# One half of the query-state product copied out of PSUM by ScalarE, the second mask built later, and a new order on all engines, in a layer of Hedgehog linear attention and a dense block

## Chip, cores and metric

The kernel runs on one core of one Trainium2 chip. The metric is the device time of one execution in microseconds. A core has TensorE (PE), VectorE (DVE), ScalarE (ACT), GpSimd (POOL) and SyncE (SP, which here only issues DMAs); each takes its instructions in order and waits on semaphores for the others.

## The reference, cut to what matters

```python
def _A_ref(x, wqkv, w_phi, wo):                   # x: 1 x 2048 x 640, 32 heads of 20
    q, k, v = split((x @ wqkv))                   # each 32 heads x 2048 x 20
    pq = einsum("bhsd,hdf->bhsf", q, w_phi)
    pk = einsum("bhsd,hdf->bhsf", k, w_phi)
    phi_q = concat([softmax(pq), softmax(-pq)])   # 40 features
    phi_k = concat([softmax(pk), softmax(-pk)])
    kv = einsum("bhsf,bhsd->bhfd", phi_k, v)      # one 40 x 20 state per head
    z  = einsum("bhsf->bhf", phi_k)
    num = einsum("bhqf,bhfd->bhqd", phi_q, kv)
    den = einsum("bhqf,bhf->bhq", phi_q, z)[..., None] + 1e-6
    return (num / den) joined over heads @ wo

h  = x + _A_ref(layernorm(x), A_wqkv, A_w_phi, A_wo)
h2 = h + silu(layernorm(h) @ B_w1) @ B_w2         # 640 -> 1728 -> 640
```

Inputs and weights are bf16. The attention is not causal: all keys go into one state per head before any query is answered.

## The kernel before

The 2048 tokens are 16 tiles of 128. Token tiles form four groups of four for the transposed activations XnT and EqT, and five groups (0-1, 2-5, 6-9, 10-13, 14-15) for the dense block. All work is cut into small words, such as `dp.3` (an operation and its tile), and one string, ORDER, lists them. Each word calls a function `op_<name>`, whose instructions are appended to the queues of the engines that they use. So each engine runs the words that concern it in the order of the string, nothing is reordered, and the semaphores are placed by the layer below, from what each instruction reads and writes. The number behind an `@` is the PSUM bank (of eight) where a word's product starts; letters at the end choose an engine (`v` VectorE, `a` ScalarE, `p` GpSimd; `q` and `b` split a kn between GpSimd and VectorE). DMAs go out on SyncE's queue (`.s`) or ScalarE's (`.a`).

The start: lx, lk, lp, lv load x, the key and value weights and w_phi. wm is a run of matmuls on constants; wt transposes a piece of the key weights on TensorE, wc copies it out; ph makes a block-diagonal form of w_phi with a first mask (mk); fk multiplies the two into Wfk, and fc (ScalarE) copies it out. mc builds a second mask, maskR, on GpSimd (a memset and four selects, lines 207 to 215); mo writes ones into the ten Vp tiles; mt transposes maskR into maskS on VectorE and copies a column of it into KVBD on GpSimd.

Key and value stage, for each tile: st takes the statistics (VectorE), rs the reciprocal root (GpSimd, lines 272 to 283), xn normalizes, xt and xc transpose by TensorE or xd by a DMA. kp and vp multiply with Wfk and the value weights (line 364); ke takes both exps (ScalarE), kr the sums and reciprocals (VectorE), kn normalizes (GpSimd, in part VectorE), vc copies the values out, and cc adds the tile into the state, which stays in PSUM bank 7. gk and gc make Wfq as fk and fc make Wfk, from transposed query weights (lq). When the last cc is done, kc copies the state out, VectorE transposes it (KVF), and km masks it into KVBD.

Query stage: qp multiplies Wfq with a group's XnT (10 matmuls of 512 columns, or 5 where there is a single row block), qe takes both exps from PSUM into EqT (ScalarE, line 461), and dp multiplies EqT with KVBD into four PSUM banks: 40 matmuls in strips of 32 rows (line 486). The result holds the positive half A[0] and the negative half A[1] side by side in each of these banks. dw then combines them, and stands unchanged in both kernels; before, every dw has `how="p"`:

```python
    def op_dw(t, how="p"):
        ...
        nc.vector.reciprocal(w[:], A[1][:, :, :, 21])                                  # L500
        nc.vector.tensor_tensor(w[:], w[:], A[0][:, :, :, 21], op=ALU.mult)            # L501
        if how == "c":
            kept = wk2().tile([P, 4, 8, 21], F32, name="kept", bufs=1)
            nc.scalar.copy(kept[:], first)                                             # L504
            first = kept[:]
        ...
        nc.vector.tensor_tensor(u[:], A[1][:, :, :, 0:21], w..., op=ALU.mult)          # L507
        nc.vector.tensor_tensor(u[:], u[:], first, op=ALU.add)                         # L510
```

Here `first` is A[0] in PSUM. dr takes the reciprocal of the denominators (rd, line 515), do multiplies each half of the heads by it (line 521, VectorE or GpSimd), td transposes the result by a DMA, op multiplies with wo, oa adds the residual (line 557), sq takes the sum of squares (ScalarE), sr the statistics (GpSimd, five or six small instructions), hn normalizes, hd transposes by a DMA.

Dense block, by group: up multiplies with w1 into two banks, ua takes Silu on ScalarE (line 649, with a table load before the first), yp and yh multiply with w2, yo and yz add the residual and store.

Of the kernel before, what the change touches and what calls it, by code (L numbers as in the profile page):

```python
# [30 lines left out]
rs.3.4 st.10 vc.1.a xn.3.v xn.8.a vp.0@0 vc.0.a vp.2@4 vc.2.a xt.3@2 xc.3.a xn.9.v st.11 rs.10.12 xn.11.a
lx.4.8.s kp.2@6 st.7 ke.2 vp.3@0 lx.12.16.s kp.3@4 ke.3 xd.9 kp.9@2 st.6 xd.8 vp.8@6 xn.10.v rs.6.8 vc.3.a
xd.10 xn.6.a lq.4.s st.4 st.5 rs.4.6 xn.4.a ke.9 xn.5.a kr.0 kr.1 kn.0.p vp.9@4 vc.9.a kp.8@0 kn.1.p xd.11
vc.8.a st.13 xn.7.a kr.9 kn.9.p kp.10@2 ke.10 st.12 rs.12.14 kr.3 kn.3.p ke.8 vp.10@4 vc.10.a xd.6 kr.8
kn.8.p vp.6@6 vc.6.a kr.2 lq.3.s xn.13.a vp.11@2 vc.11.a xd.4 vp.4@0 vc.4.a kp.4@4 lq.2.s gk.2@6 st.15 xd.5
gk.1@2 kp.5@0 st.14 xd.7 ke.4 kr.4 gc.2.a xn.12.a kp.6@4 cc.3 gc.1.a ke.5 cc.0 ke.6 cc.8 cc.9 rs.14.16
xn.14.a mt kr.5 cc.1 kn.2.q lq.0.s xd.13 kp.13@2 ke.13 kr.13 l1.0.s l1.1.s vp.5@0 vc.5.a xn.15.v kr.10 xd.12
kn.5.p kn.13.q vp.13@4 vc.13.a xd.14 kp.12@2 ke.12 kr.12 kn.10.p kp.11@0 ke.11 kr.6 vp.7@4 vc.7.a gk.4@2
vp.12@0 kn.4.q l2.0.2.s l2.2.4.s gc.4.a gk.3@4 gc.3.a kp.14@2 vp.14@4 vc.14.a kn.12.p cc.2 cc.5 kr.11 ke.14
cc.4 cc.10 vc.12.v kr.14 kn.11.q xd.15 kp.15@4 ke.15 kp.7@2 lo.0.2.s lo.2.5.s kn.14.p gk.0@0 gc.0.a kr.15  # L40
# [5 lines left out]
do.4.0.p qe.2.2 qp.3.2@5 op.1@6 qe.3.2 dp.5@0 oa.1 sq.1 l2.8.10.s l2.10.13.s op.2@4 qp.3.1@6 qe.3.1 dw.5.p
do.4.1.p td.4 sr.1 dp.9@0 hn.1.v lh.s oa.2 dr.5 dw.9.p do.5.0.p sq.2 op.3@4 oa.3 do.5.1.p op.4@6 oa.4 dp.7@0
dw.7.p dr.7 hd.1 up.0.2@4 ua.0.2 dr.6 up.0.3@6 ua.0.3 do.6.0.v dr.9 sq.4 dp.8@0 do.6.1.p up.0.1@4 ua.0.1
do.9.0.p dw.8.p sq.3 dr.8 sr.2 hn.2.a td.5 op.5@6 do.8.1.p oa.5 do.8.0.v sq.5 dp.13@0 dw.13.p up.0.0@4
ua.0.0 td.6 op.6@6 do.9.1.v oa.6 hd.2 dp.12@0 dr.13 do.7.1.v sr.4 hn.4.a sr.5 yp.1.0@4 sr.3 td.9 yp.0.1@6  # L50
dw.12.p hn.3.a td.8 do.7.0.p td.7 yh.0.0 hd.4 hn.5.v hd.5 do.13.1.p dp.11@0 dw.11.p dr.11 hd.3 yp.0.0 yo.0
yp.1.1 yo.1 op.7@0 dp.15@2 oa.7 dr.12 do.12.0.v sq.7 sr.7 op.8@6 sq.6 oa.8 do.13.0.v sr.6 hn.6.a op.9@0 oa.9
td.13 dw.15.p do.12.1.p td.12 up.1.0@6 dr.15 do.15.0.v up.1.6@0 ua.1.0 ua.1.6 dp.10@2 sq.9 hn.7.v do.15.1.v
td.15 sr.9 hn.9.v hd.9 up.1.4@6 ua.1.4 dw.10.p dr.10 do.10.0.p hd.6 up.1.3@0 op.12@6 ua.1.3 op.13@2 oa.13
do.10.1.p op.15@4 sq.8 td.10 up.1.2@0 oa.12 hd.7 sr.8 do.11.1.v hn.8.v ua.1.2 up.1.1@2 ua.1.1 hd.8 up.1.5@6
ua.1.5 up.2.6@0 oa.15 dp.14@2 dw.14.p up.2.3@6 ua.2.6 sq.13 up.2.2@0 ua.2.2 do.11.0.v sq.15 sq.12 td.11
op.10@2 oa.10 up.2.1@4 ua.2.1 dr.14 do.14.0.v up.2.5@0 ua.2.5 yp.5.0@2 ua.2.3 up.2.0@4 sr.12 hn.12.v ua.2.0
hd.12 sr.13 hn.13.a op.11@0 oa.11 hd.13 sr.15 hn.15.v up.2.4@6 hd.15 sq.10 sr.10 hn.10.a ua.2.4 yp.2.0@4
yp.4.0@0 sq.11 yp.3.1@6 sr.11 yh.1.0 hd.10 hn.11.v hd.11 yh.1.1 yp.4.1 yo.4 yp.2.1 yo.2 yp.5.1 up.3.3@0
yp.3.0 ua.3.3 do.14.1.p td.14 up.3.2@4 ua.3.2 op.14@0 oa.14 yo.5 up.3.0@4 yo.3 up.3.6@0 yh.2.1@2,6 ua.3.0  # L60
ua.3.6 up.3.4@4 sq.14 sr.14 hn.14.a hd.14 yp.9.0 yp.9.1 yo.9 up.3.5@0 ua.3.5 up.3.1@6 yp.6.0@0 ua.3.4 ua.3.1
yp.12.0@4 yp.12.1 yp.10.1@6 yp.7.1 yp.7.0 yo.7 yp.6.1 yh.2.0@2 yo.6 yh.3.0 yp.8.0 yp.8.1 yo.8 up.4.2@0
ua.4.2 up.4.1@2 ua.4.1 yo.12 up.4.0@4 yp.11.0@0 ua.4.0 up.4.3@2 ua.4.3 yp.14.0@4 yp.15.1@2 yp.10.0 yo.10
yp.14.1 yp.15.0 yh.4.0 yo.15 yo.14 yh.3.1@6,7 yp.11.1 yo.11 yp.13.0 yz.13.0.s yp.13.1 yz.13.1.a
"""

@with_exitstack
def kernel(
# [448 lines left out]

    def op_do(t, a, eng):
        if ("o", t) not in tl:
            tl["o", t] = wk2().tile([P, D], BF16, name="o", bufs=5)  # L520
        (nc.vector if eng == "v" else nc.gpsimd).tensor_tensor(  # L521
            tl["o", t][:, a * 320 : (a + 1) * 320].rearrange("p (h f) -> p h f", f=DH),
            tl["u", t][:, a, :, 0:DH],
            tl["rd", t][:, a, :].unsqueeze(2).to_broadcast([P, 16, DH]),
            op=ALU.mult,
        )
# [213 lines left out]
```

## Time and profile before

| what | value |
|---|---|
| median of 3 runs | 239.14 us (238.87 to 239.17) |
| the profiled execution, its own time | 238.86 us |
| its span, first to last instruction | 237.2 us |
| busy: PE, DVE, ACT, POOL | 229.9, 133.7, 114.9, 92.9 us |
| granted TensorE clock | 1.00 |
| first kp / first dp / first up / first yp | 10.65 / 69.27 / 96.37 / 108.0 us |

Stages by the span: start until 10.65 us, keys and values until about 67, queries and the attention's output overlapping the dense block from about 96, dense block to the end. Busy times overlap between engines. A line of the chain gives start, length and what ran; a group of instructions gives the line, the engine, the operation, tiles, shapes and count, then busy time and mean nanoseconds, then the engine's idle time before it with its releaser.

### The profile page before, as it was taken

To read this page: it belongs to the slowest core of one execution; us is meant where nothing else is said; L and a number is where in the kernel's file an instruction comes from. 1 tells how busy PE (TensorE), PEld (TensorE's weight loads), DVE (VectorE), ACT (ScalarE), POOL (GpSimd) and SP (SyncE) were. 2 spreads that over 40 slices of the span, in tenths; PEclk is the share of its full clock that TensorE was granted. 3 is DMA by queue.
4 is the path that set the end of the run, shared out by engine and by line. 5 is a ranking of instruction groups with operands and counts; after the bars stand their busy time and mean duration, and the time that the engine had idled before them with its cause. 6 is when DMAs were issued, how large, how long until landed. Compare 5 with 4: busy or idle time off the path is not lost.

```text
span 237.2 us, 6320 instructions
## 1 busy us (share of the span) xinstructions
PE 229.9 (97%) x2672; PEld 147.6 (62%) x2672; DVE 133.7 (56%) x257; ACT 114.9 (48%) x172; POOL 92.9 (39%) x184
## 2 busy tenths in 40 slices
PE   6899999999999999999999999999999999999995
PEld 2677777777544555886754645556654657688762
DVE  3899999899838989988878504321203000220032
ACT  3788998866866575664054254654014240013000
POOL 7656897798923454188071600534000100000000
PEclk9999999999999999999999999999999999999999
DMA  7964768495001849123734411103211100020012
GB/s 209 305 239 92 128 118 184 120 249 175 3 6 31 179 80 197 37 53 62 113 83 86 83 30 28 29 12 75 72 41 55 28 28 3 28 83 3 0 60 83
DMA packets 44845, 20.68 MB, mean 87 GB/s; under 512 B 34448, under 2 KB 44304, under 8 KB 44816
## 3 DMA queue, kind: packets, MB, share of 16 engines
q1 hardware_dynamic: 43728, 19.88, 36.1%
q10 hardware_dynamic: 1088, 0.39, 0.7%
q8 instruction: 21, 0.34, 0.6%
q14 instruction: 8, 0.07, 0.1%
HBM read 9.61 MB, written 2.62 MB: 52 GB/s over the span
## 4 chain that ended last, share of the span: by engine, by line
PE 88%; DVE 4%; POOL 4%; ACT 1%; DMA 1%; issue 1%; DVEq 0%; POOLq 0%
PE mm L673 24%; PE mm L627 23%; PE mm L364 18%; PE mm L548 8%; PE mm L451 7%; PE mm L486 3%; PE mm L420 2%; ACT EqT L461 1%; DMA X<-in_A_x_dram 1%; PE mm L686 1%; DVE u L507 1%; DVE u L510 1%; PE mm L637 1%; POOL RS L275 1%; PE mm L331 1%
## 5 line engine op out<-in xcount | busy, mean ns | idle before, releaser
L627 PE MATMUL mm<-HnT,w 128*128 128x512 bf16 (+1 forms) x325 | 59.1, 337 | 0.0
L649 ACT ACTIVATE shT<-mm 128x1024 bf16<-128x1024 f32 (+2 forms) x29 | 27.7, 963 | 64.3 <-PE mm L627 48.8
L673 PE MATMUL mm<-w,shT 128*128 128x320 bf16 (+2 forms) x416 | 58.5, 299 | 0.0
L673 PEld LDWEIGHTS <-shT 128*128 128x128 bf16 x416 | 39.7, 98 | 17.7 <-issue 0.8
L627 PEld LDWEIGHTS <-w 128*128 128x128 bf16 x325 | 31.3, 98 | 22.8 <-issue 0.3
L694 DVE TENSOR_TENSOR ob<-mm,X 128x640 bf16<-128x640 f32 x15 | 12.0, 817 | 47.0 <-PE mm L673 29.3
L364 PEld LDWEIGHTS <-XnT 128*128 128x128 bf16 x320 | 30.7, 98 | 11.8 <-issue 0.2
L407 POOL TENSOR_TENSOR Ek<-Ek,Sk 128x1280 bf16<-128x1280 bf16 (+2 forms) x16 | 34.6, 2184 | 3.1 <-DVE Sk L400 2.2
L557 DVE SCALAR_TENSOR_TENSOR X<-mm,X 128x640 bf16<-128x640 f32 x16 | 13.1, 823 | 21.5 <-PE mm L548 21.3
L397 DVE TENSOR_REDUCE Sk<-Ek 128x64 f32<-128x1280 bf16 x16 | 23.3, 1456 | 1.6 <-ACT Ek L389 1.6
L548 PE MATMUL mm<-wo,ot 128*128 128x320 bf16 x160 | 23.9, 299 | 0.2 <-ACT EqT L461 0.2
L521 POOL TENSOR_TENSOR o<-u,rd 128x320 bf16<-128x320 f32 x20 | 14.7, 752 | 22.7 <-DVE rd L515 14.4
L364 PE MATMUL mm<-Wfk,XnT 128*128 128x320 bf16 x160 | 23.4, 299 | 0.0
L451 PE MATMUL mm<-XnT,Wfq 128*128 128x512 bf16 x100 | 23.3, 380 | 0.0
L461 ACT ACTIVATE EqT<-mm 128x1024 bf16<-128x1024 f32 (+1 forms) x24 | 19.6, 884 | 7.4 <-PE mm L451 7.4
L364 PE MATMUL mm<-wv,XnT 128*128 128x320 bf16 x160 | 23.2, 299 | 0.0
L389 ACT ACTIVATE Ek<-mm 128x640 bf16<-128x640 f32 x32 | 20.6, 710 | 3.2 <-PE mm L364 2.7
L548 PEld LDWEIGHTS <-ot 128*128 128x128 bf16 x160 | 15.4, 98 | 7.4 <-issue 0.7
L565 ACT ACTIVATE sq<-X 128x640 bf16<-128x640 bf16 x16 | 11.7, 730 | 9.3 <-DVE X L557 7.7
L267 DVE BATCH_NORM_STATS2 stats<-X 128x6 f32<-128x320 bf16 x32 | 13.7, 468 | 3.8 <-DMA X<-in_A_x_dram 3.8
L577 POOL TENSOR_SCALAR hm<-hst,hm 128x1 f32<-128x1 f32 x16 | 4.6, 290 | 28.0 <-ACT sq L565 27.0
L451 PEld LDWEIGHTS <-Wfq 128*128 128x128 bf16 x100 | 9.1, 98 | 9.9
(78 smaller groups left out, 214.0 us busy)
## 6 DMA issues: line engine op xcount, KB each, us to landing
out_dram<-ob SPq DMA_DIRECT2D x15, 160.0 KB, 1.8
w<-in_B_w_dram SPq DMA_DIRECT2D x6, 360.0 KB, 5.2
X<-in_A_x_dram SPq DMA_DIRECT2D x3, 640.0 KB, 6.6
...
```

The source lines that it names most:

```text
L267: nc.vector.bn_stats(stats[:, k, :], X[:, t, k * 320 : (k + 1) * 320])
L364: nc.tensor.matmul(ps[:, half, 0:320], tok(XnT[t // GT], t)[:, c, :], W[:, c, half * 320 : (half + 1) * 320], start=(c == 0), stop=(c == C ...
L389: nc.scalar.activation(Ek[:, s, :].rearrange("p (a n) -> p a n", a=2), tl["kp", t][:, :, 0:320], AF.Exp, scale=1.0 - 2.0 * s,)
L397: nc.vector.tensor_reduce(Sk[:], tl["ek", t][:].rearrange("p s (h f) -> p (s h) f", f=DH), axis=AX.X, op=ALU.add,)
L407: nc.gpsimd.tensor_tensor(Ek3[:, 0:n], Ek3[:, 0:n], Sk[:, 0:n].unsqueeze(2).to_broadcast([P, n, DH]), op=ALU.mult,)
L451: nc.tensor.matmul(ps[:, k, :], Wfq[:, c, r * P : (r + 1) * P], XnT[g][:, c, :], start=(c == 0), stop=(c == C - 1),)
L461: nc.scalar.activation(E[:, s, rs[0] : rs[-1] + 1, :], tl["qp", g, i][:, 0 : len(rs), :], AF.Exp, scale=1.0 - 2.0 * s,)
L521: (nc.vector if eng == "v" else nc.gpsimd).tensor_tensor(tl["o", t][:, a * 320 : (a + 1) * 320].rearrange("p (h f) -> p h f", f=DH), tl["u ...
L548: nc.tensor.matmul(ps[:, half, 0:320], tl["ot", t][:, c, :], wo[:, c, half * 320 : (half + 1) * 320], start=(c == 0), stop=(c == C - 1),)
L627: nc.tensor.matmul(ps[:, i * W : (i + 1) * W], w1[:, c, fc * P : (fc + 1) * P], HnT[g][:, c, 0:W], start=(c == 0), stop=(c == C - 1), skip ...
L649: nc.scalar.activation(sh[:, a:b], tl["up", g, k][:, 0 : b - a], AF.Silu)
L673: nc.tensor.matmul(ps, shT[g][:, fc * W + i * P : fc * W + (i + 1) * P], w2[:, fc, a:b], start=first and fc == 0, stop=last and fc == FC - ...
```

## The change

Three lines of code change: ph can run on GpSimd (and stays on VectorE in the order), and the rings of the tiles o and hn go from five buffers to four (1.3 KB a partition each); the new tile kept has one buffer of 2.7 KB a partition. All else is the string ORDER. Thirteen of the sixteen dw words become `dw.t.c`; tiles 11, 12 and 14 keep `p`. mc moves from behind ph to behind rs.14.16, mo from the front to behind ke.1, mt from behind the first cc words to just ahead of kc. Two warm-up matmuls (256 and 128 columns) are gone. All st words come ahead of the first kr. Twelve do halves on VectorE become seven. The first products are dp.1, 0, 2, 3, 4 and all start at bank 4, with the qp words between them in banks 0 to 3. The tail of the order (yp.13.0, yz.13.0, yp.13.1, yz.13.1) is the same.

```diff
 ORDER = """
...
-ph ta mc st.1 wc.0.a wt.1@2 lx.2.4.s wc.1.v fk.0@4 wt.2@3 wc.2.v lx.8.12.s wc.4.a fc.0.a fk.4@6 fc.4.a
-rs.1.2 xn.0.v fk.1@0 fc.1.a wt.3@2 wc.3.v fk.2@4 fc.2.a xt.0@3 xn.1.v xc.0.v st.2 rs.2.3 st.9 fk.3@6 fc.3.a
+wm.256@7 wt.0@0 st.0 lk.4.5.a rs.0.1 wt.4@1 ta wc.0.a lx.1.2.s lk.1.2.s lk.2.3.s ph st.1 wt.1@2 wc.1.v
+fk.0@4 rs.1.2 wc.4.a fc.0.a wt.2@3 fk.4@6 fc.4.a wc.2.v xn.0.v fk.1@0 fc.1.a lk.3.4.s wt.3@2 wc.3.v fk.2@4
+fc.2.a lx.2.4.s xt.0@3 xn.1.v fk.3@6 fc.3.a xt.1@2 xc.0.v kp.0@0 lx.8.12.s st.2 rs.2.3 xc.1.a kp.1@4 st.3
...
-vp.15@4 vc.15.a kn.15.b kn.6.p ke.7 kr.7 kn.7.b qp.0.1@0 qp.0.0@4 qe.0.1 cc.12 cc.11 cc.15 cc.13 cc.14 cc.6
-qe.0.0 qp.0.2@6 cc.7 close kc qe.0.2 qp.3.0@2 l2.4.6.s l2.6.8.s km.1 km.0 dp.0@4 dw.0.p dr.0 do.0.0.p l1.2.s
-l1.3.s qe.3.0 do.0.1.p qp.1.0@0 dp.1@2 qe.1.0 dw.1.p dr.1 do.1.1.p qp.1.1@6 dp.3@0 dw.3.p qe.1.1 do.1.0.v
-dr.3 do.3.0.p do.3.1.p qp.2.0@4 qe.2.0 dp.2@0 dw.2.p dr.2 qp.1.2@6 qe.1.2 td.0 do.2.0.p l1.4.s l1.5.s op.0@4
...
+kn.14.p vp.14@2 qp.0.1@0 qe.0.1 kn.13.b qp.0.0@4 qe.0.0 qp.0.2@6 vc.14.v cc.14 cc.13 kr.4 kn.4.b cc.4 cc.7
+mt l1.4.s kc km.0 qp.3.0@2 qe.0.2 km.1 dp.1@4 qp.1.0@0 close dw.1.c dr.1 do.1.0.p qe.3.0 dp.0@4 do.1.1.p
+td.1 qp.1.1@2 dw.0.c dr.0 do.0.0.p do.0.1.p qe.1.0 dp.2@4 dw.2.c dr.2 do.2.1.p do.2.0.p qp.3.2@0 qe.1.1
+lo.0.2.s qp.1.2@1 qe.1.2 dp.3@4 dw.3.c qe.3.2 qp.2.0@2 qe.2.0 dr.3 dp.4@4 qp.2.1@0 dw.4.c dr.4 l1.1.s qe.2.1
+td.0 op.0@2 l1.3.s oa.0 sq.0 op.1@4 oa.1 l2.8.10.s td.2 do.3.1.p dp.6@0 dw.6.c do.4.0.p do.3.0.p l1.5.s td.3
+do.4.1.p sq.1 sr.1 hn.1.v td.4 sr.0 qp.2.2@6 qe.2.2 l2.6.8.s op.2@4 oa.2 hn.0.v dp.5@0 dw.5.c qp.3.1@6
+qe.3.1 op.3@4 op.4@0 oa.3 sq.2 hd.1 dr.5 do.5.0.p sq.3 hd.0 dr.6 do.5.1.p do.6.0.p l2.0.2.s oa.4 dp.9@2
+dw.9.c do.6.1.v up.0.0@6 ua.0.0 l2.2.4.s sr.2 td.6 up.0.3@0 ua.0.3 dp.8@2 dw.8.c dr.8 up.0.1@6 ua.0.1 dr.9
+dp.13@0 dw.13.c td.5 up.0.2@4 ua.0.2 do.9.1.p do.9.0.p td.9 sq.4 dp.7@0 dw.7.c hn.2.a dr.7 do.7.1.v do.8.0.p
+dr.13 do.8.1.p td.8 op.6@6 oa.6 op.5@4 oa.5 hd.2 sr.3 hn.3.a yp.1.1@0 lh.s sr.4 hn.4.v sq.5 sr.5 op.9@2 oa.9
...
-            tl["o", t] = wk2().tile([P, D], BF16, name="o", bufs=5)
+            tl["o", t] = wk2().tile([P, D], BF16, name="o", bufs=4)
...
-        hn = wk2().tile([P, D], BF16, name="hn", bufs=5)
+        hn = wk2().tile([P, D], BF16, name="hn", bufs=4)
```

More of the change, by code (lines that the diff above doesn't have):

```diff
@@ L25 @@
 ORDER = """
-lx.0.1.a lk.0.1.s lp.a lx.1.2.s lk.4.5.a lk.1.2.s lk.2.3.s lk.3.4.s mk mo wm.512@7 wm.512@7 wm.512@7
-wm.512@7 wm.512@7 wm.512@7 wm.512@7 wm.512@7 wm.512@7 wm.256@7 wt.0@0 st.0 rs.0.1 wm.256@2 wm.128@2 wt.4@1
-ph ta mc st.1 wc.0.a wt.1@2 lx.2.4.s wc.1.v fk.0@4 wt.2@3 wc.2.v lx.8.12.s wc.4.a fc.0.a fk.4@6 fc.4.a
-rs.1.2 xn.0.v fk.1@0 fc.1.a wt.3@2 wc.3.v fk.2@4 fc.2.a xt.0@3 xn.1.v xc.0.v st.2 rs.2.3 st.9 fk.3@6 fc.3.a
-xn.2.v xt.1@2 st.8 xc.1.a rs.8.10 kp.0@0 ke.0 kp.1@4 lv.0.3.s ke.1 lv.3.5.s xt.2@3 xc.2.a vp.1@6 lq.1.s st.3
@@ L31 @@
[L31 to L40, printed above, removed]
@@ L41 @@
-vp.15@4 vc.15.a kn.15.b kn.6.p ke.7 kr.7 kn.7.b qp.0.1@0 qp.0.0@4 qe.0.1 cc.12 cc.11 cc.15 cc.13 cc.14 cc.6
-qe.0.0 qp.0.2@6 cc.7 close kc qe.0.2 qp.3.0@2 l2.4.6.s l2.6.8.s km.1 km.0 dp.0@4 dw.0.p dr.0 do.0.0.p l1.2.s
-l1.3.s qe.3.0 do.0.1.p qp.1.0@0 dp.1@2 qe.1.0 dw.1.p dr.1 do.1.1.p qp.1.1@6 dp.3@0 dw.3.p qe.1.1 do.1.0.v
-dr.3 do.3.0.p do.3.1.p qp.2.0@4 qe.2.0 dp.2@0 dw.2.p dr.2 qp.1.2@6 qe.1.2 td.0 do.2.0.p l1.4.s l1.5.s op.0@4
-do.2.1.p td.1 oa.0 td.3 dp.4@0 dw.4.p sq.0 sr.0 qp.2.1@6 qe.2.1 td.2 dr.4 qp.2.2@4 dp.6@0 hn.0.v hd.0 dw.6.p
@@ L46 @@
[L46 to L64, printed above, removed]
+lx.0.1.a lp.a mk lk.0.1.s wm.512@7 wm.512@7 wm.512@7 wm.512@7 wm.512@7 wm.512@7 wm.512@7 wm.512@7 wm.512@7
@@ new lines @@
+wm.256@7 wt.0@0 st.0 lk.4.5.a rs.0.1 wt.4@1 ta wc.0.a lx.1.2.s lk.1.2.s lk.2.3.s ph st.1 wt.1@2 wc.1.v
+fk.0@4 rs.1.2 wc.4.a fc.0.a wt.2@3 fk.4@6 fc.4.a wc.2.v xn.0.v fk.1@0 fc.1.a lk.3.4.s wt.3@2 wc.3.v fk.2@4
+fc.2.a lx.2.4.s xt.0@3 xn.1.v fk.3@6 fc.3.a xt.1@2 xc.0.v kp.0@0 lx.8.12.s st.2 rs.2.3 xc.1.a kp.1@4 st.3
+lv.0.3.s ke.0 xn.2.v xt.2@3 xc.2.a ke.1 mo lv.3.5.s vp.1@6 vc.1.a rs.3.4 xn.3.a lx.4.8.s vp.2@0 vc.2.a
+lq.0.s st.10 st.11 rs.10.12 xn.10.a st.9 vp.0@2 xt.3@4 kp.2@6 st.8 rs.8.10 lx.12.16.s xc.3.a vc.0.a xn.11.v
@@ new lines @@
+ke.2 l2.4.6.s kp.3@0 ke.3 st.5 xn.9.a vp.3@4 gk.0@2 gc.0.a xd.11 vp.11@6 vc.3.a kp.11@0 st.4 rs.4.6 xd.10
+lq.1.s kp.10@2 st.7 vc.11.a ke.11 st.6 rs.6.8 xn.5.v xd.5 vp.10@4 kp.5@6 st.15 st.14 rs.14.16 xn.15.a mc
+xn.6.v xd.6 vp.6@0 xn.8.v xd.8 ke.10 st.12 st.13 rs.12.14 kr.2 xn.4.a kn.2.q vc.10.a lq.2.s xn.13.a xn.7.v
+vc.6.a xn.14.v gk.1@2 gc.1.a vp.5@4 vc.5.a kr.10 kn.10.p vp.8@0 xd.15 vp.15@2 xn.12.a ke.5 kr.3 vc.15.a xd.7
+vc.8.a l1.2.s l2.10.13.s kn.3.p kp.15@4 ke.15 kr.1 gk.2@6 kp.8@2 gc.2.a kn.1.p kp.6@0 cc.1 ke.6 xd.9 cc.3
@@ new lines @@
+xd.14 ke.8 kr.5 xd.13 kn.5.p cc.10 kr.11 vp.9@4 vc.9.a xd.12 vp.12@0 kr.15 vc.12.a kp.12@2 kp.9@4 ke.9 cc.5
+kn.15.p lq.3.s cc.15 ke.12 cc.2 kn.11.b cc.11 l1.0.s lq.4.s kp.7@0 ke.7 kr.6 xd.4 vp.4@4 vc.4.a gk.3@2
+gc.3.a kp.13@0 kp.4@4 ke.13 vp.13@2 vc.13.a vp.7@0 vc.7.a kn.6.p lo.2.5.s kr.8 kn.8.p kr.0 kp.14@2 ke.14
+gk.4@0 gc.4.a kn.0.p cc.0 cc.6 kr.12 kr.9 kn.12.p cc.12 kr.7 cc.8 kn.9.p cc.9 ke.4 kn.7.b kr.13 kr.14
+kn.14.p vp.14@2 qp.0.1@0 qe.0.1 kn.13.b qp.0.0@4 qe.0.0 qp.0.2@6 vc.14.v cc.14 cc.13 kr.4 kn.4.b cc.4 cc.7
@@ new lines @@
+qe.3.1 op.3@4 op.4@0 oa.3 sq.2 hd.1 dr.5 do.5.0.p sq.3 hd.0 dr.6 do.5.1.p do.6.0.p l2.0.2.s oa.4 dp.9@2
+dw.9.c do.6.1.v up.0.0@6 ua.0.0 l2.2.4.s sr.2 td.6 up.0.3@0 ua.0.3 dp.8@2 dw.8.c dr.8 up.0.1@6 ua.0.1 dr.9
+dp.13@0 dw.13.c td.5 up.0.2@4 ua.0.2 do.9.1.p do.9.0.p td.9 sq.4 dp.7@0 dw.7.c hn.2.a dr.7 do.7.1.v do.8.0.p
+dr.13 do.8.1.p td.8 op.6@6 oa.6 op.5@4 oa.5 hd.2 sr.3 hn.3.a yp.1.1@0 lh.s sr.4 hn.4.v sq.5 sr.5 op.9@2 oa.9
+hn.5.v sq.9 op.8@6 oa.8 sq.8 sr.8 hn.8.a hd.3 do.7.0.v yp.1.0 sq.6 hd.4 hd.5 dp.14@2 dw.14.p dr.14 do.14.0.p
@@ new lines @@
+td.7 yh.0.0@6 yo.1 sr.6 yp.0.0 sr.9 yp.0.1 dp.10@2 dw.10.c hd.8 yo.0 up.1.1@0 hn.6.a op.7@2 oa.7 do.14.1.p
+hn.9.v hd.9 do.13.0.p hd.6 do.13.1.p up.1.6@4 ua.1.1 dp.11@0 dw.11.p up.1.0@6 ua.1.6 ua.1.0 td.13 up.1.2@4
+sq.7 ua.1.2 td.14 dp.12@0 sr.7 dw.12.p hn.7.a hd.7 dr.11 do.11.1.p up.1.5@6 do.11.0.v op.13@4 oa.13 sq.13
+op.14@0 dr.12 oa.14 sr.13 sq.14 sr.14 up.1.4@2 td.11 hn.14.v ua.1.5 ua.1.4 up.2.3@4 ua.2.3 up.2.1@0
+do.12.1.v up.2.6@6 ua.2.1 ua.2.6 dp.15@2 dw.15.c dr.15 up.1.3@0 ua.1.3 up.2.4@6 ua.2.4 do.15.0.v up.2.0@2
@@ new lines @@
+up.2.5@4 ua.2.5 yp.4.0@0 dr.10 ua.2.0 do.12.0.p td.12 op.12@6 oa.12 up.2.2@4 ua.2.2 yp.4.1 sq.12 op.11@2
+oa.11 sq.11 yp.2.0@6 do.10.0.p do.10.1.p td.10 op.10@4 hn.13.a oa.10 sq.10 yp.7.1@2 sr.11 yh.1.0 yh.2.1@4
+sr.12 yp.2.1 yo.2 yp.7.0 do.15.1.v yp.8.1@6 yo.7 td.15 yo.4 hn.12.v sr.10 yp.3.1@2 yp.9.1 yp.5.0@0 hd.12
+hn.11.v hd.11 yp.9.0 yo.9 yp.8.0 op.15@4 oa.15 sq.15 yp.5.1 yp.3.0 hn.10.a hd.13 hd.10 yh.1.1 yo.3 yo.5
+yh.2.0@4 sr.15 yp.6.0 yp.6.1 up.3.5@2 ua.3.5 up.3.3@0 yo.8 up.3.4@6 ua.3.4 hd.14 hn.15.v hd.15 up.4.2@2
@@ L65 @@
+ua.4.2 up.3.2@6 ua.3.2 ua.3.3 yo.6 up.3.0@4 ua.3.0 up.4.1@2 up.4.0@6 ua.4.0 up.3.1@0 ua.3.1 up.3.6@4 ua.3.6
+yp.10.0@6 yp.12.1@0 yp.10.1 up.4.3@4 ua.4.3 yh.3.0 yo.10 yp.12.0 yo.12 ua.4.1 yp.15.1@4 yp.11.0@6 yh.3.1@2,3
+yh.4.0@0 yp.14.0 yp.15.0 yp.11.1 yo.15 yp.14.1 yo.14 yo.11 yp.13.0 yz.13.0.s yp.13.1 yz.13.1.a
 """
@@ L192, in op_mk, with op_ph @@
         )
-    def op_ph():
-        nc.vector.tensor_tensor(
+    def op_ph(eng="v"):
+        (nc.vector if eng == "v" else nc.gpsimd).tensor_tensor(
             phb[:],
```

## The prediction

> **What bounds the kernel now.** I read the page first, for the engine that is busy to the end; then the chain of waits, for what stops that engine; then the groups of instructions with their shapes kept apart, for prices; then the busy time by stage.
>
> ```profile
> PE 229.9 (97%) x2672; PEld 147.6 (62%) x2672; DVE 133.7 (56%) x257; ACT 114.9 (48%) x172; POOL 92.9 (39%) x184
> PE 88%; DVE 4%; POOL 4%; ACT 1%; DMA 1%; issue 1%; DVEq 0%; POOLq 0%
> ```
>
> TensorE is the bound nearly everywhere. The matmul work is the same after the change (only two warm-up matmuls go, and they lie in a time when TensorE waits for weights), and the number of switches between full-array and partial-array matmuls, each of which costs 0.1 us of start to start, counts 55 in both orders. So the change can only alter the time in which TensorE waits. Three places hold it before. The first is the start:
>
> ```profile
> 7.84 0.49 POOL maskR L215
> 8.33 0.43 POOL maskR L211
> 8.77 0.06 issue
> 8.82 0.38 POOL maskR L215
> 9.20 0.52 POOL RS L275
> 9.72 0.03 issue
> 9.75 0.46 DVE xn L291
> ```
>
> These are lines of the chain (start, length). GpSimd builds the second mask (maskR, word mc) ahead of the statistics of token tile 1 (RS, word rs.1.2), so xn.1 starts at 9.75 and the first long run of matmuls at 10.65. The second place is the ring of the query stage, again in the chain:
>
> ```profile
> 69.27 0.46 PE mm L486 x40
> ...
> 69.83 0.37 DVE w L500
> ...
> 70.22 0.07 DVE w L501
> ...
> 70.62 0.87 DVE u L507
> 71.49 0.02 issue
> 71.51 0.86 DVE u L510
> 72.38 0.04 issue
> 72.42 0.51 PE mm L486 x34
> ```
>
> A product dp fills four PSUM banks; VectorE takes the reciprocal, the weight w, the product u (L507) and the add (L510), and only when the add has ended do the banks come free for the next dp: 3.15 us here, then 3.02 and 3.01, where TensorE has only 2.66 us of other work (a qp of ten matmuls of 0.216, 0.1 of switch, a dp of 0.40). Beyond plain switches TensorE loses 1.9 us between 69.27 and 96.37 in five such gaps (0.53, 0.34, 0.46, 0.24, 0.33 by start to start), 0.6 at 124.4 for the same reason, and 0.2 at 40. After 125.5 it never waits.
>
> ```profile
> 69.27:96.37 27.10, 26.02 (x476) 14.14 (x477) 24.17 (x50) 17.23 (x25) 10.61 (x21) 1.00 0.55 112
> 96.37:125.15 28.78, 28.26 (x407) 20.05 (x407) 24.21 (x53) 13.25 (x21) 15.25 (x43) 1.00 0.38 72
> ```
>
> Columns: length, then busy time of PE, weight loads, DVE, ACT, POOL. What matters is the third busy time: VectorE works for 24.2 of 27.1 and 24.2 of 28.8 us. It has hardly any room in this stage.
>
> ```profile
> L507 DVE TENSOR_TENSOR u<-mm,w 128x672 f32<-128x672 f32 x16 | 13.7, 857 | 2.4 <-POOL o L521 1.3 <-DVE w L501 0.2
> L510 DVE TENSOR_TENSOR u<-u,mm 128x672 f32<-128x672 f32 x16 | 13.7, 853 | 0.6
> L168 ACT CAST Vp<-mm 128x640 bf16<-128x640 f32 x15 | 10.3, 713 | 3.8 <-PE mm L364 3.7
> L461 ACT ACTIVATE EqT<-mm 128x1024 bf16<-128x1024 f32 x16 | 15.5, 1021 | 7.4 <-PE mm L451 7.4
> L521 DVE TENSOR_TENSOR o<-u,rd 128x320 bf16<-128x320 f32 x12 | 5.8, 485 | 0.1
> ```
>
> **The copy to kept.** For thirteen tiles ScalarE copies the positive half (672 elements, f32) out of PSUM, and the add reads that copy. Its price is not in the trace. Between the 640-element cast (713 ns) and the 1024-element exp (1021 ns) the slope is 0.8 ns an element, so 0.74 us; the ends are 0.61 (the distance of two casts in a row) and 1.02. The add from SBUF lies between one 485 ns row and 2.1 of them (320 against 672 elements, 1.02); I keep 0.85, the row of the same instruction with the same shape.
>
> The decisive question is what runs beside what. In the built program of the changed kernel the copy waits for VectorE's w of the same tile, and it is u (L507), not the add, that waits for ScalarE. All three read the same four banks. So copy and product do not overlap; the copy stands between w and u. From the start of dp: reciprocal at 0.58, w done at 1.17, ScalarE told 0.08 later (VectorE's residual add to the following square takes 0.09), copy to 1.99, u 2.04 to 2.90, banks free at 2.95 instead of 3.02: nothing is won there, although the add has left PSUM. And VectorE, in order, stands still during the copy: its round is 0.59 + 0.08 + 0.74 + 0.05 + 0.89 + 0.88 + 0.27 (rd) = 3.50 us instead of 2.97. The Trainium skill, page "PSUM — Partial Sum Buffer", section "PSUM bank collisions raise a hardware error", says that two engines must not touch one bank and quadrant at once, reads included; the waits in the built program agree, and without such a rule the sum would be that of the first rival.
>
> Behind each copy on ScalarE stand the exps of the next qp, whose banks TensorE wants. Step by step from dp.1 = 0, with a pair of exps at 1.94 (512 wide: 1.09): dp.0 at 2.95; qp.1.1 waits until 3.90 for the exps of qp.3.0, which start only after copy 1; from there VectorE's round rules: dp.2 at 6.45, dp.3 at 9.95, dp.4 at 13.60 (copy 3 also waits 0.2 for exps). Without waits that is 4 x 2.66 = 10.64, so 2.96 lost. Then dp.6 loses 0.3 (residual add of tile 0 behind tile 4's late add), dp.5 0.2, qp.3.1 0.6 (its banks' exps stand behind copy 6 and a square), op.4 0.8 (banks of dp.5, whose dw stands behind hn.0, which waits for GpSimd's statistics), dp.9 0.2. Together 5.0 up to the first up matmul, where the before kernel loses 1.9: **+3.1**.
>
> In the next stretch the first Silu stands behind two squares, copy 9 and the table load (1.28), so up.0.1 waits 0.9 for its banks, and dp.7 waits 0.7 for u of tile 13: 1.6 against the 0.6 lost at 124.4: **+1.0**. From yp.1.1 on I find cover: the transposed hn of tiles 2 to 5 land some 3 us before up.1.1, and VectorE has half its time free there (16.8 of 54.9 us after 125.15). The do halves move from VectorE to GpSimd (12 down to 7, 485 ns each; GpSimd's 752): 2.4 us off VectorE, hidden in its idle time late, no term.
>
> **The start.** With mc moved behind rs.14.16, GpSimd computes rs.1.2 as soon as VectorE has the variance. xn.1 then follows wc.3 (ends 9.09) at once, ends 9.45, xt.1 at 9.50. But the five casts to Wfk on ScalarE end at 10.49 as before, and kp.0 needs the last of them in its fourth matmul: it can gain 0.5 us, not 0.9. **-0.5**, bounds 0 and -0.9. The copies of the ones into Vp (mo, 1.5 us) move to GpSimd's idle time about 13 us. The two warm-up matmuls gone leave TensorE idle for about 1.8 us instead of 1.6; the granted clock is 1.00 there before.
>
> **The key and value stage.** VectorE is the fullest engine beside TensorE (51.8 of 56.0 us). All sixteen st now come before the first kr: 25.9 + 16 rounds of 1.94 + its shares of kn, two xn and vc.14 end near 64; GpSimd's kn (34.8 us before, mc before them) end at 64 to 65.5; the last cc wants them at 65.9. Cover about 0.5 us. Without it each tenth is a tenth on the end. The transpose of the second mask (0.62, mt) stands just ahead of KVF on VectorE, beside cc.4, cc.7 and the copy kc. No term but the 0.2 us gap at 40, which goes: **-0.2**.
>
> **Sum.** The profiled execution took 238.86 (span 237.2); 238.86 + 3.1 + 1.0 - 0.5 - 0.2 = 242.3. It lies 0.28 under the median of 239.14, so I add 0.28: 242.5.
>
> **Rivals.** First, the copy is hidden: ScalarE reads beside u, or finds the tiles earlier than I trace. Then banks come free after u, at 2.11, under TensorE's 2.66, and the 2.5 us of gaps go with the 0.7 of start and cc: 239.14 - 3.2 = 235.9, or somewhat more with small new waits. For it: ScalarE is idle for 9.9 of 27.1 us. Against it: the waits above. It decides if TensorE's round (2.66) rather than VectorE's sets the distance of the first dps. 11%. Second, ScalarE becomes the bound: its 17.2 us of 27.1 rise by eight copies to 23.1, plus waits for w, and every copy can fall behind a pair of exps (1.94). If eight copies each come another 0.6 late, 4.8 more: 247.3. 7%. Third, the end of the key stage slips: last kn 1.5 us late with the rest as forecast, 244.0; 12%, inside the range. Fourth, gains and losses cancel to within 0.2%, about what a measurement of this kernel can tell from no change: 3%.
>
> **Numbers.** The forecast with its spread and the third rival hold 79%. Cheap end: copy 0.61 and cheaper add take 0.15 to 0.3 from each of some eight rounds, start 0.9: 240 or a little under. Dear end: copy 1.02 adds 0.28 to eight rounds, and a slipped key stage: 245.8. Range 239.7 to 245.8. Faster 11%, same 3%, slower 86%.
>
> **What would show it.** Right: L507 idle before it, released by ScalarE's L504; dp.1 to dp.4 some 13.6 us apart; the L504 row near 0.74 us; VectorE's idle time in this stretch up while TensorE's share falls; xn.1 near 9.1. Wrong: L507 starting within 0.1 us of w, dps 2.7 us apart, or a gap of TensorE before the last cc larger than all of these.

## The result and the profile after

The changed kernel takes 244.77 us (median of 5 runs, 244.6 to 245.04) against 239.14 us of the kernel before measured beside it: a ratio of 1.024, 95% interval 1.0226 to 1.0255. It is slower by 5.6 us, where 3.4 were forecast. The profiled execution took 245.0 us, its span 242.9 (before: 237.2).

The page of the changed kernel: busy time of the engines, and the shares of the chain of waits.

```profile
PE 231.3 (95%) x2670; PEld 148.5 (61%) x2670; DVE 133.1 (55%) x253; ACT 122.2 (50%) x183; POOL 97.7 (40%) x189
PE 74%; DVE 10%; ACT 6%; POOL 3%; issue 2%; DMA 2%; ACTq 0%; DVEq 0%; POOLq 0%
```

TensorE's busy time is nearly the same (its records overlap where matmuls run in strips), but its share of the chain falls from 88% to 74%, and ScalarE's rises from 1% to 6%. To see where, I divided both traces at the same events: the start of the first kp, of the first dp, of the first up, and the end of the last matmul.

| us | first kp at | to first dp | to first up | to the last matmul's end | sum |
|---|---|---|---|---|---|
| before | 10.65 | 58.55 | 27.10 | 138.05 | 234.35 |
| after | 10.12 | 59.97 | 29.98 | 140.01 | 240.09 |
| difference | -0.53 | +1.42 | +2.88 | +1.96 | +5.74 |

The start, in the chain of waits of the changed kernel (start, length, what):

```profile
9.31 0.35 DVE xn L291
9.67 0.40 DVE XnT L166
...
12.33 1.59 DVE xn L291
13.92 0.07 DVE RS L272
13.98 0.44 PE mm L302 x5
```

xn.1 stands at 9.31 instead of 9.75, and no mask of GpSimd stands ahead of it. But a second xn, of tile 2, is now in the chain with 1.59 us. The instruction ran from 12.24 to 13.91, 1.67 us where its shape takes about 0.4 elsewhere, and TensorE's xt.2 at 13.98 comes 0.91 us late by start to start (its distance from the start of the matmul before it, less what that distance is without a wait). Beside it GpSimd ran the ten memsets of mo, as the timeline shows (start, length, engine, line, what):

```profile
12.22 1.51 POOL L204 MEMSET Vp<- 128x32 bf16 x10
12.24 1.67 DVE L291 TENSOR_SCALAR xn<-X,MV,RS 128x640 bf16<-128x640 bf16 x1
```

The end of the key stage, from the same chain:

```profile
57.79 1.31 ACT Ek L389 x2
...
59.19 1.50 DVE Sk L397
...
60.71 0.56 DVE Sk L400
...
61.44 3.27 POOL Ek L407 x2
...
65.34 1.86 POOL Ek L407
67.20 0.04 issue
67.25 0.66 PE mm L420 x64
```

The exps of key tile 14 (ke.14), their sums on VectorE (kr.14), and the last three kn instructions of GpSimd follow each other, and the last one ends at 67.20. cc.4 waits for it, 0.52 us by start to start.

The ring of the query stage, again in the chain:

```profile
71.53 0.73 ACT kept L504
...
72.28 0.87 DVE u L507
...
73.18 0.87 DVE u L510
...
74.07 0.35 DVE rd L515
74.43 0.22 DVE w L500
...
74.67 0.20 DVE w L501
...
74.97 0.73 ACT kept L504
```

Copy, product, add, the two reciprocals, the next w and the next copy stand in one row, each begun within 0.1 us of the end of the one before: nothing here runs beside anything else on the path. One turn is 74.97 - 71.53 = 3.44 us. The groups of instructions (shapes kept apart) show the same as a wait:

```profile
L507 DVE TENSOR_TENSOR u<-mm,w 128x672 f32<-128x672 f32 x16 | 13.7, 858 | 11.9 <-ACT kept L504 10.8 <-POOL hm L574 0.9
L510 DVE TENSOR_TENSOR u<-u,kept 128x672 f32<-128x672 f32 x13 | 11.2, 863 | 0.5
L504 ACT COPY kept<-mm x13: 719/719/722, 71.5 to 150.1; 128x672 f32<-128x672 f32 x13
```

(The last line is from the view of the tile kept: shortest, median and longest in ns.) VectorE stands idle 11.9 us ahead of u, 10.8 of them for the copy; before it was 2.4. In the stretch from the first dp to the first up, the busy times (PE, weight loads, DVE, ACT, POOL) are:

```profile
70.10:100.08 29.98, 25.69 (x436) 14.45 (x436) 21.18 (x46) 21.59 (x32) 10.48 (x21) 1.00 0.55 118
```

Before, VectorE was busy for 24.2 of 27.1 us there. Now no engine is full: 25.7, 21.2 and 21.6 of 30.0. That is what a ring of dependences looks like, as against an engine that is the bound.

### The profile page after: what moved, and what is told of

It is laid out like the page before. It is cut to its first block, busy times and chain, and to the rows that moved or that the text cites. A ratio compares the mean times of both kernels' runs of the same rounds, so it can differ in the third digit from the quotient of the medians.

```text
span 242.9 us, 6341 instructions
## 1 busy us (share of the span) xinstructions
PE 231.3 (95%) x2670; PEld 148.5 (61%) x2670; DVE 133.1 (55%) x253; ACT 122.2 (50%) x183; POOL 97.7 (40%) x189
## 4 chain that ended last, share of the span: by engine, by line
PE 74%; DVE 10%; ACT 6%; POOL 3%; issue 2%; DMA 2%; ACTq 0%; DVEq 0%; POOLq 0%
PE mm L673 24%; PE mm L627 19%; PE mm L364 16%; PE mm L548 7%; ACT kept L504 3%; DVE u L507 3%; POOL Ek L407 2%; DMA wk<-in_A_wqkv_dram 2%; DVE u L510 1%; PE mm L451 1%; ACT EqT L461 1%; PE mm L486 1%; PE mm L420 1%; PE mm L686 1%; PE mm L637 1%
## 5 line engine op out<-in xcount | busy, mean ns | idle before, releaser
L627 PE MATMUL mm<-HnT,w 128*128 128x512 bf16 (+1 forms) x325 | 58.3, 337 | 0.7 <-ACT shT L649 0.7
L694 DVE TENSOR_TENSOR ob<-mm,X 128x640 bf16<-128x640 f32 x15 | 11.9, 817 | 52.7 <-PE mm L686 30.3
L364 PEld LDWEIGHTS <-XnT 128*128 128x128 bf16 x320 | 30.7, 98 | 11.9 <-issue 0.3
L407 POOL TENSOR_TENSOR Ek<-Ek,Sk 128x1280 bf16<-128x1280 bf16 (+2 forms) x16 | 34.2, 2169 | 2.4 <-DVE Sk L400 2.1
L521 POOL TENSOR_TENSOR o<-u,rd 128x320 bf16<-128x320 f32 x25 | 18.6, 765 | 36.6 <-DVE rd L515 26.6
L507 DVE TENSOR_TENSOR u<-mm,w 128x672 f32<-128x672 f32 x16 | 13.7, 858 | 11.9 <-ACT kept L504 10.8
```

What stands on the lines that cost most here:

```text
L364: nc.tensor.matmul(ps[:, half, 0:320], tok(XnT[t // GT], t)[:, c, :], W[:, c, half * 320 : (half + 1) * 320], start=(c == 0), stop=(c == C ...
L407: nc.gpsimd.tensor_tensor(Ek3[:, 0:n], Ek3[:, 0:n], Sk[:, 0:n].unsqueeze(2).to_broadcast([P, n, DH]), op=ALU.mult,)
L507: nc.vector.tensor_tensor(u[:], A[1][:, :, :, 0:21], w[:].unsqueeze(3).to_broadcast([P, 4, 8, 21]), op=ALU.mult,)
L521: (nc.vector if eng == "v" else nc.gpsimd).tensor_tensor(tl["o", t][:, a * 320 : (a + 1) * 320].rearrange("p (h f) -> p h f", f=DH), tl["u ...
L627: nc.tensor.matmul(ps[:, i * W : (i + 1) * W], w1[:, c, fc * P : (fc + 1) * P], HnT[g][:, c, 0:W], start=(c == 0), stop=(c == C - 1), skip ...
```

## The experiments

### What the copies cost, and what the new order

`e1_all_p` takes the copies of all thirteen tiles out and leaves all else as changed.

```diff
-... dp.1@4 qp.1.0@0 close dw.1.c dr.1 ...
+... dp.1@4 qp.1.0@0 close dw.1.p dr.1 ...
...
```

> The changed kernel with all thirteen copies taken out again (every dw adds from PSUM), the new order untouched. Theory A (the copy stands between w and u in VectorE's round and makes it 3.43 us instead of 3.0): dp.1 to dp.4 come some 3.05 us apart, the gaps ahead of the qp words shrink, and most of the query stage's loss goes: 240.3 us, 239.6 to 241.5. Rival B (the new order itself is what costs, whatever dw does): within 0.7 us of the changed kernel's 244.8.

Measured: 240.73 us, ratio 1.0065 (1.0037 to 1.0093). So the copies cost 4.0 us, and the order by itself some 1.5. The chain shows the ring without a copy:

```profile
73.22 0.53 PE mm L486 x38
...
73.77 0.37 DVE w L500
...
74.16 0.20 DVE w L501
...
74.39 0.87 DVE u L507
...
75.28 0.86 DVE u L510
...
76.18 0.53 PE mm L486 x33
```

A turn is 76.18 - 73.22 = 2.96 us: u follows w after 0.03 us. By the same division, e1 has its first kp at 10.01, then 59.93, 27.10 and 139.17. So the query stretch is as long as before the change, to the hundredth; the copies make all of its +2.88 and 0.84 of the +1.96 behind it. The order makes +1.4 in the key stage and +1.1 behind the first up. Behind the first up TensorE's waits in e1 sum to 1.44 us by start to start, against 0.68 before; that is 0.8 of the 1.1, and the rest is not explained here.

### How the copy costs: order on VectorE, or the queue on ScalarE

`e2_two_halves` keeps the copies, but cuts copy and product in two by PSUM banks and lets each engine begin with the other half.

```diff
-nc.scalar.copy(kept[:], first)
...
-nc.vector.tensor_tensor(u[:], A[1][:, :, :, 0:21], w..., op=ALU.mult)
+for j in range(2):
+    a, b = slice(2 * j, 2 * j + 2), slice(2 - 2 * j, 4 - 2 * j)
+    nc.scalar.copy(kept[:, a], first[:, a])
+    nc.vector.tensor_tensor(u[:, b], A[1][:, b, :, 0:21], w[:, b]..., op=ALU.mult)
```

> The changed kernel with copy and product cut in two by banks: ScalarE copies banks 0 and 1 of a product while VectorE multiplies banks 2 and 3, then the other way round, so neither waits for a bank that the other reads. Theory A: the first half of u starts within 0.1 us of w, VectorE's round falls to about 2.9 us, dp words come 2.9 to 3.05 apart, and the time falls to 241, 240.0 to 242.3. Rival C (it is ScalarE's time, not the waiting of u, that costs): ScalarE has 26 copies of some 0.45 us instead of 13 of 0.72, about 2.3 us more work, and the time stays at 244.5 to 246.5.

Measured: 242.5 us, 1.013 (1.0112 to 1.0149), just above theory A's range and far below the rival's. The timeline of three engines (start, length; in brackets the idle time of the engine before, and what ended it; L508 is u there and L517 the add):

```profile
74.10 1.06 DVE L508 TENSOR_TENSOR u<-mm,w 128x336 f32<-128x336 f32 x2
74.18 0.96 ACT L507 COPY kept<-mm 128x336 f32<-128x336 f32 x2
74.25 2.32 PE L451 MATMUL mm<-XnT,Wfq 128*128 128x512 bf16 x10 [1.31 <-ACT EqT L461]
75.03 1.95 ACT L461 ACTIVATE EqT<-mm 128x1024 bf16<-128x1024 f32 x2
75.26 0.86 DVE L517 TENSOR_TENSOR u<-u,kept 128x672 f32<-128x672 f32 x1
```

Copy (2 x 440 ns) and product now run side by side, within 1.06 us. The gaps ahead of the dps went. What is left is on TensorE's line: a qp that waits 1.31 us for its banks (the largest of four such waits: 1.31, 0.07, 0.87 and 0.92 us), because the exps of the qp before stand behind the copies on ScalarE. `e4_exps_first` undoes only this in the changed kernel, without the halves:

```diff
-dw.1.c dr.1 do.1.0.p qe.3.0
+qe.3.0 dw.1.c dr.1 do.1.0.p
...
-dw.0.c dr.0 do.0.0.p do.0.1.p qe.1.0
+qe.1.0 dw.0.c dr.0 do.0.0.p do.0.1.p
...
-dw.2.c dr.2 do.2.1.p do.2.0.p qp.3.2@0 qe.1.1
+qe.1.1 dw.2.c dr.2 do.2.1.p do.2.0.p qp.3.2@0
...
-dw.3.c qe.3.2
+qe.3.2 dw.3.c
```

> The changed kernel with the exps of qe.3.0, 1.0, 1.1 and 3.2 put ahead of the copies of tiles 1, 0, 2 and 3 on ScalarE. Theory A (VectorE's round rules, the exps behind the copies only show where TensorE stands when it waits): the gaps of 0.55 us ahead of qp.1.1, qp.3.2 and qp.2.0 go, those ahead of the dp words grow by as much, the time stays at 244.8, 244.0 to 245.8. Rival D (the exps held up behind the copies are a cost of their own): three or four gaps of 0.55 us go, 242.6 to 243.2.

Measured: 245.55 us, 1.0272 (1.0235 to 1.0309). The gaps of 0.65 ahead of the qps are gone, and the ones ahead of the dps grew from 0.53, 0.33, 0.33, 0.40 to 1.03, 0.87, 0.87, 0.94. Its timeline:

```profile
75.28 0.19 DVE L501 TENSOR_TENSOR w<-w,mm 128x32 f32<-128x32 f32 x1
75.58 0.72 ACT L504 COPY kept<-mm 128x672 f32<-128x672 f32 x1 [0.67 <-DVE w L501]
76.33 0.86 DVE L507 TENSOR_TENSOR u<-mm,w 128x672 f32<-128x672 f32 x1 [0.86 <-ACT kept L504]
```

The ring w, copy, u, add is the limit; the wait only changed its place. Both edits together are `e7_halves_exps_first`:

> The changed kernel with copy and product cut in two by banks and also the exps of qe.3.0, 1.0, 1.1 and 3.2 ahead of the copies. With the halves alone TensorE still lost 1.5, 0.2, 1.0 and 1.1 us ahead of qp words, whose banks wait for exps behind copies. Theory I (once VectorE's round is short, the order on ScalarE is the next bound): those gaps fall by 1.5 to 2.5 us in all, but u's second half now waits for a copy behind exps, so some comes back ahead of dp: 241.5 us, 240.7 to 242.0. Rival J (ScalarE's added work as such is the bound): 242.5, within 0.4.

Measured: 240.97 us, 1.0088 (1.0068 to 1.0107), within 0.3 us of the kernel without copies (0.5 by the two ratios). Its query stretch is 27.41 us, and 139.06 follow. The two causes lie one behind the other: the halves alone give 2.3 us, the exps alone nothing, and after the halves the exps give another 1.5 (by the traces the query stretch falls from 28.85 to 27.41 us). But a copy that is hidden gives nothing either: e1's 27.10 is still shorter.

### The same copies in the old order

`e3_before_c` puts `c` in the place of `p` for the same thirteen tiles in the kernel before.

```diff
-dp.0@4 dw.0.p dr.0
+dp.0@4 dw.0.c dr.0
...
-            tl["o", t] = wk2().tile([P, D], BF16, name="o", bufs=5)
+            tl["o", t] = wk2().tile([P, D], BF16, name="o", bufs=4)
...
-        hn = wk2().tile([P, D], BF16, name="hn", bufs=5)
+        hn = wk2().tile([P, D], BF16, name="hn", bufs=4)
```

> The kernel before, its order untouched, with the copy in the same thirteen tiles (and four buffers of o and hn, as there). Theory A: every round of VectorE in the query stage is 0.43 us longer and some eight of them are on the path: 242.5 us, 241.3 to 244. Rival B (the copy is free, only the new order costs): within 0.5 us of 239.1.

Measured: 254.55 us, 1.0637 (1.0614 to 1.0659). Both expectations missed; theory A was too low by 12 us. The timeline at the worst place:

```profile
97.78 1.94 ACT L461 ACTIVATE EqT<-mm 128x1024 bf16<-128x1024 f32 x2 [1.62 <-PE mm L451]
99.61 0.73 ACT L504 COPY kept<-mm 128x672 f32<-128x672 f32 x1
100.37 0.86 DVE L507 TENSOR_TENSOR u<-mm,w 128x672 f32<-128x672 f32 x1 [4.63 <-ACT kept L504]
...
101.28 0.63 PE L486 MATMUL mm<-KVBD,EqT 32*128 32x44 bf16 x40 [3.53 <-DVE u L507]
```

In the old order the copy of tile 5 stands behind the exps of qp.3.1 on ScalarE, which wait for TensorE. VectorE stands still for 4.63 us and TensorE for 3.5. During TensorE's wait the granted clock fell (length, the five busy times, then the clock, the DMA share and GB/s):

```profile
99.80:106.60 6.80, 3.96 (x53) 2.45 (x53) 5.27 (x11) 1.98 (x4) 1.41 (x2) 0.50 0.23 38
```

It was 1.00 ahead of it and behind it. The Trainium skill, page "TensorE: Matmul & The Clock Gate", Part 1, gives half rate after an idle window of about 3.4 us; this trace has the half rate, for 6.8 us, but it begins 2.1 us after the last matmul ahead of the wait had ended (97.75), so the length of that window is not borne out here. The next twenty matmuls of op, most of them at the lower clock, take 4.52 us, where twenty of the same shape take 2.88 in the changed kernel. The query stretch is 38.38 us, 11.3 longer. The rings of o and hn are down to four buffers here, as in the changed kernel, but no wait of L521 or of hn in this trace is put down to a transposing DMA, which would be the sign of a buffer too few. So the new order was a help to the copies: at this place it spares them the wait behind exps. Without it the copies, with the fall of the clock that they bring, cost 15 us, with it 4.0.

### The order's own loss: mo beside xn, and the end of the key stage

`e5_mo_front` and `e8_all_p_mo_front` move mo back to where it was before, to the front, in the changed kernel and in e1.

```diff
-lp.a mk lk.0.1.s
+lp.a mk mo lk.0.1.s
...
-ke.1 mo lv.3.5.s
+ke.1 lv.3.5.s
```

> The changed kernel with the ten memsets of ones (mo) on GpSimd at the front again, ahead of the first statistics. Theory E (in the changed kernel xn.2 on VectorE took 1.67 us instead of 0.39 because the memsets ran on GpSimd at the same time, and TensorE waited 0.91 us for it ahead of xt.2): xn.2 takes about 0.4 us, the gap goes, 244.8 - 0.9 = 243.9 us, 243.5 to 244.2. Rival F (xn.2 was long for another reason, such as the residue of DMA or ScalarE work): xn.2 stays over 1 us and the time at 244.8, within 0.3.

> The new order without any copy, and with the memsets at the front: what is left of the change is order alone. Theories A and E together: 240.7 - 0.9 = 239.8 us, 239.5 to 240.2, level with the kernel before or a little slower. Rival: the two losses hide each other and the time stays at 240.5 or above.

Measured: 244.72 us (1.0236, 1.0222 to 1.0249) and 240.75 us (1.0081, 1.0057 to 1.0105). (In the profiled execution of e5 the first kp comes only at 11.57 us, in that of e10 below at 11.68; so stretches are counted from the first kp.) No gain in either, though xn.2 took 0.39 us and xt.2's wait of 0.9 was gone in both. All of it came back ahead of cc.4: 1.52 us in e5 and 1.41 in e8, in place of 0.52. The reason is one instruction of VectorE, its half of kn.7, here in e1, in e8 and in e5, in e1 and e8 with the GpSimd instruction that ran when it was issued:

```profile
53.09 2.35 POOL L407 TENSOR_TENSOR Ek<-Ek,Sk 128x1280 bf16<-128x1280 bf16 x1
55.19 0.93 DVE L411 TENSOR_TENSOR Ek<-Ek,Sk 128x640 bf16<-128x640 bf16 x1
```

```profile
54.23 2.35 POOL L407 TENSOR_TENSOR Ek<-Ek,Sk 128x1280 bf16<-128x1280 bf16 x1
54.37 2.90 DVE L411 TENSOR_TENSOR Ek<-Ek,Sk 128x640 bf16<-128x640 bf16 x1
```

```profile
55.71 3.01 DVE L411 TENSOR_TENSOR Ek<-Ek,Sk 128x640 bf16<-128x640 bf16 x1
```

The same instruction takes three times as long. GpSimd works through its own kn (L407) at that time, each 2.35 us. In e1 the half was issued at 55.19, 0.24 us before a GpSimd instruction ended (55.43); it was done at 56.12, and GpSimd's next took 2.94 instead of 2.35. In e8 it was issued at 54.37, 0.1 us after the last GpSimd instruction had ended and a new one had begun (54.23 to 56.58). It ended 0.68 us after that one. So the two don't run side by side here; one stands until the other's instruction is over. The Trainium skill, page "SBUF — State Buffer", section "Who interferes with whom", says that VectorE shares its second port pair with GpSimd under an exclusive lock, and that a VectorE instruction with two inputs in SBUF contends with a GpSimd instruction that reads SBUF. These runs agree, with 0.93 against 2.90 us. The xn beside the memsets looks the same: it was issued 0.02 us after the first of the ten and ended 0.18 us after the last. That the memsets are what held it, e5 and e8 show (0.39 us without them); that it is the same lock, no run here shows.

To test it, kn.7.b becomes kn.7.p (GpSimd does the whole tile, L411 of that tile goes) in e8, in e5 and, as a control, in e1, where the half had met no collision:

```diff
-ke.4 kn.7.b kr.13
+ke.4 kn.7.p kr.13
```

> The kernel of e8 (no copies, mo at the front) with one word changed: kn.7.b becomes kn.7.p, so GpSimd scales the whole key tile 7 and VectorE's half of it (L411) goes. Theory L (the loss at the end of the key stage is the collision of this one L411 with GpSimd's L407: 2.90 us in e8, begun at 54.37 just after a GpSimd instruction of 54.23 to 56.58, instead of 0.93 in e1): the last kr then follows ke.14 (ends 58.12) at once instead of starting at 59.16, the last kn ends some 0.85 us earlier, cc.4 waits about 0.5 us instead of 1.4, and the time is 239.9 us (239.5 to 240.2). Rival M (the stage is bound by the sum of VectorE's and GpSimd's work, the order's fault as a whole): GpSimd has 1.1 us more to do, cc.4 waits 1.4 us or more, 240.75 us or above.

> The changed kernel with mo at the front (e5) and kn.7.p for kn.7.b. Theory L: L411 of tile 7 (3.01 us in e5, 0.93 in the changed kernel) is gone, cc.4 waits 0.5 to 0.6 us instead of 1.5, 243.85 us (243.5 to 244.2). Rival M: no gain, 244.7 us or above.

> Control: the kernel of e1 (no copies, mo late as in the change) with kn.7.p for kn.7.b. There L411 of tile 7 met no collision (0.93 us) and the last kr waits for ScalarE's ke.14, so theory L expects no change: cc.4 waits 0.5 us, 240.7 us (240.4 to 241.0). If simply less work on VectorE is what gains, it is 240.2 us or below; if GpSimd's sum binds, 241.5 or above.

Measured: e9 240.36 us (1.0068, 1.0045 to 1.0092), e10 244.54 (1.0225, 1.0212 to 1.0238), e11 241.16 (1.0089, 1.0076 to 1.0102). In the place that the theory speaks of all three agree with it. cc.4 waits 0.52 us in each, and from the first kp to the first dp there are 59.01 us in e9 (e8: 59.90), 59.02 in e10 (e5: 59.90) and 59.97 in the control (e1: 59.93): 0.9 us less where there was a collision, nothing where there was none, though GpSimd has more work in all three. The times show less of it, and lie between the two expectations (the intervals of e9 and e10 overlap those of e8 and e5, so the times alone don't tell them apart): behind the first up the three take 0.3 to 0.7 us more than their counterparts (the wait ahead of dp.7 is 0.89 instead of 0.52 in e9 and 0.89 instead of 0.58 in the control), and e9 and e11 take another 0.3 us between the last matmul and the end. Why, these runs don't settle; that the control has it too shows that it does not come from the collision.

`e12_halves_mo_kn7p` joins all that was found: halves, exps first, mo at the front, kn.7.p.

> What the change could have been, with all that was learned: copies kept, but copy and product by halves over different PSUM banks and the four exps ahead of copies (e7, 240.97 us), mo at the front and kn.7.p. Theory L: 0.9 us less than e7, 240.1 us (239.7 to 240.5), still above the kernel before. Rival M: 241 us or above.

Measured: 239.73 us, 1.0035 (1.0023 to 1.0047): 1.2 us less than e7, at the lower end of what theory L gave, and without the later loss of e9 to e11 (139.05 behind the first up, e7 139.06). Of the 5.6 us of the change some 4.9 are undone with the copies still in, and it is still slower than before.

### The one part that pays

`e6_before_mc_later` takes the kernel before and moves only the second mask.

```diff
-ph ta mc st.1
+ph ta st.1
...
-rs.1.2 xn.0.v
+rs.1.2 mc xn.0.v
```

> The kernel before with one word moved: the second mask (mc) behind rs.1.2 on GpSimd instead of ahead of it. Theory G (the mask holds up xn.1 by 0.7 us, and ScalarE's cast to Wfk lets 0.3 to 0.5 of that reach the end): 238.7 us, 238.5 to 238.9, faster than before by 0.1 to 0.3%. Rival H (the start is made by the weights' DMA and by ScalarE's casts, or the mask's instructions slow VectorE where they now run): 239.1, within 0.2, or slower.

Measured: 238.15 us, ratio 0.9966 (0.9954 to 0.9979), faster than both kernels, with the whole interval below 1, and by more than theory G gave (238.5 to 238.9). The chain at the start, to be held against that of before:

```profile
8.83 0.48 PE mm L331 x6
9.31 0.32 PE mm L302 x5
9.63 0.53 PE mm L364 x3
10.16 0.01 issue
10.17 0.84 PE mm L364 x5
```

No GpSimd, no VectorE: TensorE goes from Wfk through xt.1 to kp.0 without a pause, but for the one ahead of kp.0's fourth matmul (0.17 by start to start), which waits for the last cast to Wfk. The first kp is at 9.58 instead of 10.65. I had expected the cast to hold it at some half a microsecond of gain; the cast came earlier too in this execution, in which the next piece of the key weights was on hand 0.36 us earlier (TensorE's matmuls on it begin at 5.88 instead of 6.24). So of the 1.07 us at the first kp not all is shown to be the mask's; the medians differ by 0.86.

## Why the prediction came out as it did

**The copy between w and u: right, in mechanism and size.** The copy took 0.719 us (forecast 0.74), VectorE's turn 3.43 (3.50), dp.1 to dp.4 13.47 (13.6, from 70.10 to 83.57), the add from SBUF 0.858 (0.85: leaving PSUM gains nothing, the row from PSUM has 0.853). e1, e2 and e4 show that it is the overlap with u that is lacking: e2 gives the overlap back and the gaps ahead of the dps go; e4 only moves the queue and nothing is gained. The forecast for the query stretch and what follows was +4.1; by the division above it is +2.88 +1.96 = +4.84, of which e1 puts 3.7 on the copies and 1.1 on the order.

**The term "op.4 0.8" was mis-sized.** It took 1.60 us (96.33 to 98.07). The prediction let the banks of dp.5 wait for GpSimd's statistics and hn.0, and that chain is in the trace as traced; but behind w there comes once more a copy (96.40, 0.73 us) ahead of u. Without that copy the wait would have been some 0.85 us (1.60 less the copy and the 0.03 us ahead of u), which is the term; so this copy looks to have been left out, though the prediction does not show the working of that term. Smaller: dp.7 0.99 instead of 0.7, dp.5 0.35 instead of 0.2, qp.3.1 0.44 instead of 0.6, up.0.1 0.88 as forecast (0.9); the 0.3 ahead of dp.6 did not come.

**"From yp.1.1 on I find cover": not quite.** Two waits remain there, 0.17 us at 124.6 and 0.26 at 126.7. e1 has them as well (0.17 and 0.34), so they are the order's, not the copies'.

**The start: right for the mask, wrong for mo.** The first kp is at 10.12, 0.53 earlier, held by the cast as forecast (its fourth matmul waits 0.21). That mo moves "to GpSimd's idle time about 13 us" at no cost was wrong: idle on GpSimd is not free for VectorE. xn.2 took 1.67 us instead of 0.39, and TensorE lost 0.91.

**The key stage: "cover about 0.5 us" was a lack of 0.52 us.** The path named was the right one (GpSimd's kn at the end), and the 0.17 us at 40 went as forecast. The sum on VectorE was too short because ke.14, on ScalarE, and not VectorE's own work, sets kr.14 (59.19, after VectorE had been idle for 0.97 us), and the first of GpSimd's last three kn instructions waits for kr.14. That chain begins on TensorE, with kp.14 from 56.19 to 57.71, and so it moves with TensorE: the 0.52 us stays in e9 and e12, where xt.2 waits no more. With xt.2 this makes +1.42 instead of -0.2: 1.6 of the 2.3 us by which the forecast was short of the result. The rest is the 0.75 of the copy's stretch.

**The rivals.** The hidden copy is out: in the ring u starts only when the copy has ended. ScalarE as the bound is out: it is busy for 21.6 of 30.0 us, and e4 shows that its queue alone is worth nothing. Gains and losses did not cancel. The slip of the key stage, at 12% and 244.0 us, came nearest to what happened; the mo part of it I had not seen. That the result lies inside the range is in part luck: the dear end was made of a dearer copy and a slipped key stage, and the copy was not dearer; the room was taken up by xt.2, which stood in no term, by cc.4 and by op.4. The dear end was also added short: 0.28 us on eight rounds and the 1.5 us of the third rival make 246.2, not 245.8.
